# Chunk attention followed by a SoLU feed-forward layer: the start's order written anew in finer pieces, the scaling of six tiles' probabilities moved to GpSimd, and fewer warming products

## The chip, the cores and the metric

The kernel runs on one core of one Trainium2 chip. The metric is the device time of one execution in microseconds (us), the median of several runs.

## The reference

The first part is attention in chunks of 64 positions: no position sees another chunk. Its output, heads side by side, is the input of a feed-forward layer whose activation is SoLU (h times its own softmax) with a normalisation behind it.

```python
# q, k, v: 8 batches x 8 heads x 576 positions x 64 (float32)
scores = (1 / sqrt(64)) * matmul(q_c, k_c^T)              # per chunk of 64
attn   = exp(scores - max(scores)); attn = attn / (sum(attn) + 1e-9)
out    = matmul(attn, v_c)
x      = out as 4608 tokens x 512
h      = x @ w_in                                         # 512 -> 1024
solu   = h * (exp(h - max(h)) / (sum(exp(h - max(h))) + 1e-9))
ln     = (solu - mean(solu)) / sqrt(var(solu) + 1e-6) * g_ln
result = ln @ w_out                                       # 1024 -> 512
```

The weights w_in and w_out come as 64-bit floats.

## The kernel before, in words

The 4608 tokens are 36 tiles of 128. One tile holds two chunks of 64 positions. Every tile passes through the same steps, and the kernel names each step with a letter. `n` loads q and k of a tile, `v` loads v. `N:i:0` and `N:i:1` turn q and k of tile i on TensorE (four 128x128 transposes each into a bank of PSUM) and evict them to qT and kT. `S` makes the scores. `A` subtracts the maximum (VectorE) and takes the exp (ScalarE), `B` sums, inverts and scales with the inverse. `T` turns the probabilities on TensorE and ScalarE evicts them to attn_t in four copies; from tile 6 on `U` turns them on VectorE and brings them to attn_t with eight DMA loads (four issued by SyncE, four by GpSimd). `V` multiplies with v and splits the result into a high part x_h (an eviction with rounding) and a low part x_l (a subtraction on VectorE).

`M` is the input product of a tile: 24 matmuls of 512 columns, since x and w_in are each split into a high and a low part and three of the four pairings are summed. `X` takes the maximum of its 1024 sums (h_nmax, VectorE) and the exp (ScalarE). `Y` multiplies sums and exp on VectorE (z, with its sum) and then shifts by the mean on ScalarE, or on GpSimd where the step is listed. `R` forms the variance: eps and sq on ScalarE, then the tiny u and r on GpSimd. The turned z comes by TensorE for tiles 0 and 1 (`z`) and from tile 2 on by VectorE (`Z`, z_b) and 16 DMA loads to z_t. `F` is a third of the output product, 8 matmuls of 24, and `o` scales and stores a tile.

The weights come in eight pairs of rows, `P:0` to `P:7` (four of w_in, four of w_out). For each pair x, `c:x` clamps the high words of the 64-bit floats (w_a, on GpSimd) and lets ScalarE shift their range (Prelu); `b:x` converts the low words (w_b); `C:x` joins both (w_a, VectorE); `t:x` rounds to the high part (ScalarE), `d:x` subtracts for the low part (VectorE). `G` makes g_sb from g_ln. `w:n` issues n warming products on TensorE, which multiply the identity matrix and are not used.

Everything up to tile 5's input product is written out as a list of such words, `START` (lines 18 to 31). A word that appears again resumes its step where it yielded. Each engine works through its instructions strictly in the order in which the list makes them, and so does each DMA queue. `MOVED` (lines 34 to 37) names the steps that run on another engine than usual. The nat buffer that `n` fills has two places, so a load of tile i waits until tile i-2 is turned. Behind the list, from line 775 on, a loop over tiles 5 to 35 runs two tiles per turn, and each input product is followed by the scores and values of coming tiles and by thirds of an output product.

The functions that the steps of the change touch are `load_natural`, `load_v`, `turn_natural`, `unit_high`, `unit_low`, `softmax_a`, `softmax_b`, `ffn_in` and `warm`.

Of the kernel before, what the change touches and what calls it, by code (L numbers as in the profile page):

```python
# [15 lines left out]


START = """
n:0 w:3 N:0:0 N:0:0 w:1 N:0:1 N:0:1 g w:1 S:0 A:0 G P:0 P:0 n:1 A:0 c:0 c:0 w:3 N:1:0 N:1:0 w:1
N:1:1 b:0 N:1:1 G P:1 w:1 S:1 B:0 v:0 C:0 A:1 t:0 T:0 T:0 c:1 c:1 w:4 V:0 V:0 P:2 b:1 c:2 n:2  # L20
d:0 P:3 A:1 n:3 w:6 N:2:0 w:1 N:2:1 C:1 V:0 B:1 t:1 c:2 T:1 N:2:0 b:2 N:2:1 T:1 d:1 S:2 n:4
M:0 M:0 C:2 t:2 c:3 c:3 v:1 A:2 A:2 b:3 d:2 C:3 N:3:0 N:3:1 N:3:1 M:0 N:3:0 S:3 N:4:0 B:2 N:4:1
t:3 N:4:0 A:3 P:5 d:3 c:5 N:4:1 A:3 T:2 T:2 S:4 V:1 M:0 P:4 n:5 B:3 T:3 V:1 V:1 M:1 X:0 X:0 T:3
A:4 A:4 b:4 v:2 N:5:1 c:4 n:6 P:7 c:5 N:5:0 c:4 Y:0 Y:0 n:7 N:5:1 V:2 b:5 v:3 B:4 N:5:0 V:2 b:7
C:4 z:0:1 P:6 v:5 N:6:0 X:1 v:4 C:5 N:6:0 S:5 Q:2 q:8 t:4 V:2 d:4 N:6:1 N:6:1 X:1 t:5 A:5 Y:1
M:2 z:0:1 z:0:1 X:2 A:5 R:0 z:0:0 z:0:0 q:8 N:7:1 q:8 c:6 S:6 Y:1 V:3 X:2 T:4 T:4 z:0:0 d:5 F
V:3 Y:2 Y:2 N:7:0 A:6 c:6 c:7 V:3 b:6 B:5 C:6 n:8 N:7:0 M:3 R:1 c:7 q:8 N:7:1 C:7 T:5 z:1:0 t:6
T:5 S:7 t:7 d:6 X:3 X:3 d:7 V:4 V:4 Y:3 Y:3 R:2 z:1:1 A:6 F F A:7 V:4 z:1:0 z:1:0 v:6 Z:2 A:7
M:4 F B:7 Z:3 o:0 V:5 z:1:1 z:1:1 B:6 F F v:7 O:0 X:4 N:8:0 X:4 U:6 U:7 V:5 Y:4 V:5 K:9 Y:4 N:8:0
R:4 R:3 N:8:1 N:8:1 o:1  # L30
# [32 lines left out]
def chunk_attention_then_solu_ffn(  # L63
# [420 lines left out]
    def ffn_in(i):  # L486
# [2 lines left out]
        ph = st[i, "h"] = pool_h.tile([P, 2, HALF], F32, name="ph")  # L489

        sums = [(n, cc, m) for n in range(2) for cc in range(NCC) for m in range(3)]
        if i == 0:
# [388 lines left out]
```

## Time and profile before

| | |
|---|---|
| runs | 472.53, 472.22, 471.87 us; median 472.22 |
| the profiled execution | 473.01 us |
| its span (first to last instruction) | 471.2 us |
| TensorE matmuls | 461.9 us busy, 98% |
| VectorE | 374.1 us, 79% |
| ScalarE | 256.4 us, 54% |
| GpSimd | 147.6 us, 31% |
| granted TensorE clock | 1.00 in all slices |

The profile is one execution. Busy times are sums over instructions. A matmul's end is modelled and matmuls overlap, so two that follow each other in 0.23 us each show about 0.39 us. A chain of waits is followed back from the last instruction to whatever released it. A row of a timeline gives start, duration, engine, operation, what is written from what, and in brackets how long the engine stood idle before it and who ended that. Rows of one engine may overlap by some hundredths of a microsecond.

### The profile page before, as it was taken

What the parts mean: (1) busy time and instruction counts of PE and PEld (TensorE: products, weight loads), DVE (VectorE), ACT (ScalarE), POOL (GpSimd) and SP (SyncE); (2) the same over time, 40 slices, a digit from 0 to 9 for tenths busy, and PEclk for the clock granted to TensorE, in tenths of its full rate; (3) what the DMA queues carried; (4) which work ended last, traced back from release to release, by engine and by line L of the source; (5) the groups of instructions that cost most, each with busy time, mean ns of one, the idle gap of its engine ahead of it and who ended that gap; (6) DMA issues with size and microseconds to landing.
All of it is one profiled execution on the core that took longest, in us unless ns stands there. A gap on an engine that the chain in (4) does not pass through costs nothing.

```text
span 471.2 us, 11062 instructions
## 1 busy us (share of the span) xinstructions
PE 461.9 (98%) x4212; PEld 380.9 (81%) x4212; DVE 374.1 (79%) x521; ACT 256.4 (54%) x422; POOL 147.6 (31%) x298
## 2 busy tenths in 40 slices
PE   8999999999999999999999999999999999999997
PEld 6677778788888888888888888888888888888886
DVE  3999999797869887878788878797979797954441
ACT  2979984555544646464645455554555554545451
POOL 2212716151505050505050505042514141424430
PEclk9999999999999999999999999999999999999999
DMA  9999999878786878687258496948743535343231
GB/s 244 313 278 217 216 138 179 176 184 150 194 140 170 154 181 162 167 154 177 70 144 167 134 175 157 180 126 173 160 112 105 121 91 136 85 118 96 73 95 50
DMA packets 192924, 72.57 MB, mean 154 GB/s; under 512 B 177188, under 2 KB 177960, under 8 KB 191976
## 3 DMA queue, kind: packets, MB, share of 16 engines
q1 hardware_dynamic: 186200, 58.89, 57.3%
q0 software_dynamic: 6528, 12.86, 10.3%
q8 instruction: 33, 0.54, 0.5%
q14 instruction: 19, 0.16, 0.1%
q10 hardware_dynamic: 144, 0.13, 0.1%
HBM read 36.70 MB, written 9.44 MB: 98 GB/s over the span
## 4 chain that ended last, share of the span: by engine, by line
PE 85%; DMA 5%; DVE 3%; ACT 3%; SPq 2%; issue 1%; DVEq 0%; ACTq 0%
PE po L54 39%; PE ph L54 37%; PE tp L54 5%; PE sx L54 4%; SPq L54 2%; DMA nat<-in_q_dram 2%; DMA v_sb<-in_v_dram 2%; ACT z L54 1%; DMA attn_t<-a_b 1%; ACT attn_t L54 1%; ACT wo_h L54 1%; DVE z_b L54 1%; DVE z L54 0%; DVE s_sum L54 0%; ACT sq L54 0%
## 5 line engine op out<-in xcount | busy, mean ns | idle before, releaser
L54 ACT ACTIVATE z<-ph,h_nmax 128x1024 f32<-128x1024 f32 x36 | 40.2, 1118 | 139.1 <-DVE h_nmax L54 139.1
L54 PE MATMUL po<-wo_l,z_h 128*128 128x512 f32 (+1 forms) x288 | 113.0, 392 | 0.0
L54 PE MATMUL ph<-wi_l,x_h 128*128 128x512 f32 x288 | 112.8, 392 | 0.0
L54 PE MATMUL ph<-wi_h,x_h 128*128 128x512 f32 x288 | 112.2, 389 | 0.0
L54 PE MATMUL po<-wo_h,z_l 128*128 128x512 f32 (+1 forms) x288 | 111.6, 388 | 0.0
L54 PE MATMUL po<-wo_h,z_h 128*128 128x512 f32 (+1 forms) x288 | 111.4, 387 | 0.0
L54 POOL DMA_DIRECT2D z_t<-z_b x144 | 71.8, 506 | 27.0 <-DVE z_b L54 21.9
L54 PE MATMUL ph<-wi_h,x_l 128*128 128x512 f32 x288 | 78.1, 390 | 0.0
L54 POOL TENSOR_TENSOR u<-ssq,eps 128x1 f32<-128x1 f32 x36 | 6.8, 189 | 213.3 <-ACT sq L54 213.1
L54 DVE TENSOR_REDUCE h_nmax<-ph 128x1 f32<-128x1024 f32 x36 | 44.0, 1222 | 31.3 <-PE ph L54 31.2
L54 PEld LDWEIGHTS ph<-wi_h,x_l 128*128 128x128 f32 x288 | 53.9, 188 | 11.6 <-DVE x_l L54 0.4
L54 PEld LDWEIGHTS po<-wo_l,z_h 128*128 128x128 f32 x288 | 54.1, 188 | 11.4
L54 PEld LDWEIGHTS ph<-wi_l,x_h 128*128 128x128 f32 x288 | 54.1, 188 | 11.5 <-ACT x_h L54 0.2
L54 PEld LDWEIGHTS po<-wo_h,z_l 128*128 128x128 f32 x288 | 54.1, 188 | 11.1
L54 PEld LDWEIGHTS ph<-wi_h,x_h 128*128 128x128 f32 x288 | 54.1, 188 | 11.0
L54 PEld LDWEIGHTS po<-wo_h,z_h 128*128 128x128 f32 x288 | 54.1, 188 | 10.5
L54 DVE TENSOR_TENSOR z_l<-z_t,z_h 128x1024 fp32r<-128x1024 f32 (+1 forms) x37 | 42.0, 1136 | 20.9 <-ACT z_h L54 17.7
L54 DVE SCALAR_TENSOR_TENSOR z<-ph,z 128x1024 f32<-128x1024 f32 x36 | 44.1, 1224 | 13.3 <-ACT z L54 13.2
L54 ACT ACTIVATE z<-z,z_sum 128x1024 f32<-128x1024 f32 x33 | 38.1, 1155 | 22.9 <-DVE z L54 21.7
L54 DVE STREAM_TRANSPOSE z_b<-z 128x1024 f32<-128x1024 f32 x34 | 41.2, 1212 | 7.2 <-DMA v_sb<-in_v_dram 3.3
L54 ACT CAST z_h<-z_t 128x1024 fp32r<-128x1024 f32 (+1 forms) x37 | 36.0, 972 | 8.5 <-PE po L54 4.9
L54 ACT ACTIVATE o_sb<-po,r 128x512 f32<-128x512 f32 (+1 forms) x36 | 24.3, 674 | 24.7 <-POOL r L54 18.6
(76 smaller groups left out, 589.8 us busy)
## 6 DMA issues: line engine op xcount, KB each, us to landing
out_dram<-o_sb SPq DMA_DIRECT2D x35, 256.0 KB, 2.5
v_sb<-in_v_dram SPq DMA_DIRECT2D x32, 256.0 KB, 4.3
z_t<-z_b POOLq DMA_DIRECT2D x128, 64.0 KB, 2.8
z_t<-z_b SPq DMA_DIRECT2D x128, 64.0 KB, 3.0
q_st<-in_q_dram SPq DMA_DIRECT2D x96, 72.0 KB, 3.3
k_st<-in_k_dram SPq DMA_DIRECT2D x96, 72.0 KB, 3.1
w_raw<-in_moe_w_out_dram SPq DMA_DIRECT2D x4, 1024.0 KB, 7.5
attn_t<-a_b POOLq DMA_DIRECT2D x60, 64.0 KB, 3.8
```

The source lines that it names most:

```text
L54: ins = make(*args, **kwargs)
```

## The change

- The list for tiles 0 to 8 is written anew. The order of every engine and of the DMA queues changes up to tile 5's input product; the loop behind it stays.
- Steps yield more often, so that the list can put other words between their parts: `softmax_a` (between maximum and subtraction), `softmax_b` (after the sum and after the inverse), `unit_high` and `unit_low` of a pair of w_out (between their two halves), `ffn_in` of tiles 1 to 4 (every six products, as tile 0 before). Tile 1's products are sorted like tile 0's, by rows of w_in, and within these the products with x_l last. In the loop the same steps run as a whole.
- `softmax_b` scales on GpSimd for tiles 0 to 5 (`B:i=pool`).
- Evictions of N:0:1, N:2:0, V:0 and V:5 go to VectorE; those of N:0:0, N:8:0 and N:8:1 go to ScalarE. Conversion b:5 goes to GpSimd and b:7 to VectorE. The shift by the mean of tile 2 goes to GpSimd, that of tile 1 to ScalarE.
- 11 warming products instead of 21, all into one accumulator tile.
- `queue_of` could move loads to another queue; no load is listed in `MOVED`, so all stay on SyncE.

```diff
 START = """
-n:0 w:3 N:0:0 N:0:0 w:1 N:0:1 N:0:1 g w:1 S:0 A:0 G P:0 P:0 n:1 A:0 c:0 c:0 w:3 N:1:0 N:1:0 w:1
...
+n:0 P:0 P:0 c:0 w:1 w:1 w:1 n:1 w:1 N:0:0 N:0:0 N:0:1 n:2 c:0 w:1 N:0:1 S:0 A:0 A:0 b:0 P:1 N:1:0
...
 MOVED = """
-N:0:0=dve N:8:0=dve N:8:1=dve Y:0=pool Y:1=pool Y:3=pool b:7=pool c:0=pool c:1=pool c:2=pool
-c:3=pool c:4=pool c:5=pool c:6=pool c:7=pool
+Y:0=pool Y:3=pool c:0=pool c:1=pool c:2=pool c:3=pool c:4=pool c:5=pool c:6=pool c:7=pool N:0:1=dve
+B:0=pool V:0=dve N:2:0=dve B:1=pool B:2=pool B:3=pool b:5=pool B:4=pool Y:2=pool B:5=pool V:5=dve
 """
...
+    def queue_of(word):
+        return {"pool": pool, "act": act}.get(moved.get(word), sync)
...
             for y in range(2):
+                if y:
+                    yield
                 g = g_sb[:, 2 * m + y:2 * m + y + 1]
...
         dve.tensor_reduce(
             out=nmax, in_=sv, axis=AX.X, op=ALU.max, negate=True
         )
+        yield
...
         dve.tensor_reduce(out=ssum, in_=ES[i % 2], axis=AX.X, op=ALU.add)
+        yield
         rinv = small.tile([P, H], F32, name="s_rinv")
         dve.reciprocal(out=rinv, in_=ssum)
+        yield
         a = st[i, "e"] = work.tile([P, H, CH], F32, name="s_e") if i < PE_TURNED else e
-        dve.tensor_tensor(
+        (pool if f"B:{i}" in moved else dve).tensor_tensor(
             out=a, in0=e, in1=rinv.unsqueeze(2).to_broadcast([P, H, CH]), op=ALU.mult,
         )
...
-        if i == 0:
-            sums.sort(key=lambda s: s[1])
+        if i < 2:
+            sums.sort(key=lambda s: (s[1], s[2] == 2))
...
-            if i == 0 and at and at % 6 == 0:
+            if i < first and at and at % 6 == 0:
                 yield
...
+    warmed = []
+
     def warm(n):
         m = ident.unsqueeze(1).to_broadcast([P, 2, P])
-        ph = ps_h.tile([P, 2, HALF], F32, name="ph")
+        if not warmed:
+            warmed.append(ps_h.tile([P, 2, HALF], F32, name="ph"))
+        ph = warmed[0]
```

ScalarE at the very beginning, before (kT is N:0:1's eviction, e0 the exp of tile 0, w_a the Prelu of pair 0, qT and the second kT the evictions of tile 1):

```order
L54 COPY kT_111<-tp_120 128x512
L54 ACTIVATE e0_97<-e0_97 128x8x64
L54 ACTIVATE w_a_157<-w_a_157 128x1024
L54 COPY qT_164<-tp_166 128x512
L54 COPY kT_165<-tp_174 128x512
L54 CAST wi_h_90<-w_a_157 128x1024
```

The same place with the change (qT_118 is N:0:0's eviction, qT_159 and kT_160 are those of tile 1):

```order
L55 COPY qT_118<-tp_120 128x512
L55 ACTIVATE w_a_109<-w_a_109 128x1024
L55 COPY qT_159<-tp_161 128x512
L55 ACTIVATE e0_97<-e0_97 128x8x64
L55 COPY kT_160<-tp_167 128x512
L55 CAST wi_h_90<-w_a_109 128x1024
```

The exp of tile 0 moved from ahead of the Prelu to behind it and behind the eviction of N:1:0.

SyncE's DMA issues at the seam between list and loop, before (z_t are the loads of tiles 2 and 3, attn_t those of tiles 6 and 7):

```order
L54 DMA k_st<-in_k_dram 32x18x32 x8
L54 DMA v_sb<-in_v_dram 128x8x64
L54 DMA z_t<-z_b 32x512 x8
L54 DMA v_sb<-in_v_dram 128x8x64
L54 DMA out_dram<-o_sb 128x512
L54 DMA attn_t<-a_b 32x512 x4
```

With the change:

```order
L55 DMA k_st<-in_k_dram 32x18x32 x16
L55 DMA z_t<-z_b 32x512 x8
L55 DMA attn_t<-a_b 32x512 x4
L55 DMA v_sb<-in_v_dram 128x8x64
L55 DMA out_dram<-o_sb 128x512 x2
```

The load of v and the first store moved from ahead of the attn_t loads to behind them.

GpSimd at the same seam, before (u and r of tile 2 stand first, those of tiles 4 and 3 follow behind the loads):

```order
L54 TENSOR_SCALAR z<-z,z_sum 128x1024
L54 TENSOR_TENSOR u<-ssq,eps 128x1
L54 TENSOR_TENSOR r<-u,mhalf 128x1
L54 DMA z_t<-z_b 32x512 x8
L54 DMA attn_t<-a_b 32x512 x4
```

With the change (s_e is the scaling of tile 5):

```order
L55 TENSOR_TENSOR s_e<-e_98,s_rinv 128x512
L55 TENSOR_SCALAR z<-z,z_sum 128x1024
L55 DMA z_t<-z_b 32x512 x8
L55 TENSOR_TENSOR u<-ssq,eps 128x1
L55 TENSOR_TENSOR r<-u,mhalf 128x1
L55 TENSOR_TENSOR u<-ssq,eps 128x1
L55 TENSOR_TENSOR r<-u,mhalf 128x1
L55 DMA attn_t<-a_b 32x512 x4
```

u and r of tiles 2 and 3 moved between the z_t loads and the attn_t loads.

## Rows read from the trace of the kernel before

**Rows 1.** Chain of waits, end of the start: start us, us, what.

```profile
83.17 3.18 DMA attn_t<-a_b
...
88.55 5.69 PE po L54 x24
```

**Rows 2.** TensorE's timeline: start us, us, operation, count, idle before and its releaser.

```profile
16.39 2.86 PE L54 MATMUL ph<-ident 128*128 128x256 f32 x12
...
79.18 0.48 PE L54 MATMUL ph<-wi_l,x_h 128*128 128x512 f32 x1
...
84.81 0.69 PE L54 MATMUL sx<-kT,qT 64*64 64x64 f32 x32
86.59 0.96 PE L54 MATMUL sx<-attn_t,v_sb 64*64 64x64 f32 x29 [1.09 <-DMA attn_t<-a_b]
```

**Rows 3.** SyncE's timeline of DMA issues: start us, us of issuing, count.

```profile
0.73 0.45 SPq L54 DMA_DIRECT2D nat<-in_q_dram  x1
...
76.05 5.07 SPq L54 DMA_DIRECT2D z_t<-z_b  x8
...
82.59 2.43 SPq L54 DMA_DIRECT2D attn_t<-a_b  x4
```

**Rows 4.** GpSimd's timeline: pairs 2 and 6 of the weights, and attn_t.

```profile
17.47 1.57 POOL L54 TENSOR_SCALAR w_a<-w_raw 128x1024 f32<-128x1024 f32 x1 [2.66 <-DMA w_raw<-in_moe_w_in_dram]
...
52.76 1.15 POOL L54 TENSOR_SCALAR w_a<-w_raw 128x1024 f32<-128x1024 f32 x1 [0.78 <-DMA w_raw<-in_moe_w_out_dram]
...
77.73 1.97 POOL L54 DMA_DIRECT2D attn_t<-a_b  x4 [0.54 <-issue]
```

**Rows 5.** Stretches: us, busy us of PE, PEld, DVE, ACT, POOL; clock, DMA, GB/s.

```profile
466.00:472.00 6.00, 1.88 (x16) 1.67 (x14) 0.48 (x1) 0.47 (x1) 0.00 (x0) 1.00 0.12 44
...
13.59:78.54 64.95, 63.02 (x664) 50.69 (x664) 63.00 (x89) 51.28 (x93) 24.14 (x27) 1.00 1.02 220
```

**Rows 6.** VectorE's timeline, rows of the first exp, of tile 2's scaling, of tile 4.

```profile
9.65 0.16 DVE L54 TENSOR_SCALAR g_sb<-tp 128x8 f32<-128x8 f32 x1
...
11.84 1.23 DVE L54 SCALAR_TENSOR_TENSOR w_a<-w_a,w_b 128x1024 uint32<-128x1024 uint32 x1 [0.27 <-ACT w_a L54]
13.59 0.69 DVE L54 TENSOR_REDUCE s_nmax<-sx 128x8 f32<-128x512 f32 x1 [0.52 <-PE sx L54]
...
28.13 0.69 DVE L54 TENSOR_TENSOR s_e<-e,s_rinv 128x512 f32<-128x512 f32 x1
28.74 0.68 DVE L54 TENSOR_REDUCE s_nmax<-sx 128x8 f32<-128x512 f32 x1
...
77.31 1.23 DVE L54 SCALAR_TENSOR_TENSOR z<-ph,z 128x1024 f32<-128x1024 f32 x1
...
80.28 0.66 DVE L54 COPY qT<-tp 128x512 f32<-128x512 f32 x1
```

**Rows 7.** ScalarE's timeline: tile 0's exp, N:1:0's eviction, tile 4's exp, tile 3's sq.

```profile
9.17 0.63 ACT L54 ACTIVATE e<-e 128x512 f32<-128x512 f32 x1 [2.27 <-DVE e L54]
...
11.72 0.57 ACT L54 COPY qT<-tp 128x512 f32<-128x512 f32 x1
...
76.07 1.12 ACT L54 ACTIVATE z<-ph,h_nmax 128x1024 f32<-128x1024 f32 x1 [6.69 <-DVE h_nmax L54]
...
81.05 1.06 ACT L54 ACTIVATE sq<-z 128x1024 bf16<-128x1024 f32 x1
```

**Rows 8.** DMA issues of the whole run: count, KB each, median us to landing.

```profile
v_sb<-in_v_dram SPq DMA_DIRECT2D x32, 256.0 KB, 4.3
...
w_raw<-in_moe_w_in_dram SPq DMA_DIRECT2D x3, 1024.0 KB, 8.9
nat<-in_q_dram SPq DMA_DIRECT2D x8, 256.0 KB, 6.4
```

**Rows 9.** Groups by form, 0 to 88.5 us: busy us, mean ns, idle before.

```profile
L54 POOL TENSOR_SCALAR w_a<-w_raw 128x1024 f32<-128x1024 f32 x8 | 10.0, 1252 | 28.4 <-DMA w_raw<-in_moe_w_in_dram 13.2 <-DMA w_raw<-in_moe_w_out_dram 11.0 <-DVE w_a L54 4.1
...
L54 POOL TENSOR_TENSOR r<-u,mhalf 128x1 f32<-128x1 f32 x5 | 3.8, 766 | 0.4
```

More of the change, by code (lines that the diff above doesn't have):

```diff
@@ L25 @@
[L25 to L30, printed above, removed]
+n:0 P:0 P:0 c:0 w:1 w:1 w:1 n:1 w:1 N:0:0 N:0:0 N:0:1 n:2 c:0 w:1 N:0:1 S:0 A:0 A:0 b:0 P:1 N:1:0
@@ new lines @@
+w:1 N:1:1 C:0 N:2:0 n:3 N:1:0 A:0 B:0 N:1:1 S:1 N:2:0 w:1 v:0 B:0 B:0 A:1 A:1 t:0 d:0 P:2 N:2:1 w:1
+T:0 N:2:1 A:1 B:1 S:2 g T:0 v:1 c:1 c:1 w:1 P:3 B:1 A:2 N:3:0 n:4 w:1 N:3:1 N:3:0 A:2 B:1 T:1 A:2
+b:1 C:1 N:3:1 t:1 V:0 B:2 n:5 P:4 T:1 S:3 V:0 c:2 c:2 B:2 V:0 w:1 d:1 c:3 G v:2 M:0 b:2 V:1 C:2 V:1
+V:1 M:0 M:1 t:2 b:3 c:3 A:3 G N:4:0 A:3 N:4:0 M:1 C:3 N:4:1 N:4:1 N:5:0 S:4 B:2 d:2 T:2 N:5:0 Q:2
+P:5 N:5:1 A:4 t:3 d:3 M:0 M:0 M:1 A:3 A:4 T:2 B:3 c:4 A:4 N:5:1 B:3 b:4 n:6 c:4 X:0 X:0 C:4 V:2 n:7
@@ new lines @@
+S:5 Y:0 v:3 V:2 B:3 T:3 T:3 Y:0 V:2 M:1 A:5 X:1 t:4 B:4 M:2 t:4 z:0:0 P:6 z:0:0 N:6:0 X:1 v:4 A:5
+A:5 N:6:0 c:5 c:5 M:2 M:2 v:5 P:7 z:0:0 Y:1 d:4 b:5 d:4 q:8 C:5 N:6:1 z:0:1 N:6:1 z:0:1 M:2 N:7:1
+X:2 B:4 R:0 t:5 N:7:1 V:3 B:4 d:5 X:2 z:0:1 n:8 Y:2 S:6 v:6 F V:3 V:3 N:7:0 c:6 A:6 Y:1 b:6 B:5 t:5
+c:7 N:7:0 q:8 c:6 C:6 T:4 M:3 M:3 z:1:0 d:5 q:8 M:3 A:6 M:3 T:4 S:7 t:6 d:6 t:6 A:6 d:6 c:7 V:4 b:7
+C:7 R:1 t:7 t:7 X:3 d:7 F V:4 z:1:1 d:7 z:1:0 Y:2 B:5 X:3 z:1:0 B:5 F F z:1:1 A:7 Y:3 V:4 A:7 Z:2
+A:7 q:8 T:5 z:1:1 B:6 Y:3 B:7 B:7 B:6 Z:3 T:5 B:6 M:4 M:4 R:2 M:4 M:4 X:4 X:4 B:7 V:5 V:5 R:3 N:8:1
@@ L221, in unit_high @@
         else:
-            top = wo_h[:, 2 * m:2 * m + 2, :]
+            top = tops[x] = wo_h[:, 2 * m:2 * m + 2, :]
             for y in range(2):
+                if y:
+                    yield
                 g = g_sb[:, 2 * m + y:2 * m + y + 1]
@@ L238, in unit_low @@
         for y in range(2):
+            if y:
+                yield
             dve.scalar_tensor_tensor(
@@ L320, in load_natural @@
             for p0, p1, b, s in tile_parts(i):
-                sync.dma_start(
+                queue_of(f"n:{i}").dma_start(
                     nat[p0:p1, i % 2, x],
@@ L328, in load_v @@
         for p0, p1, b, s in tile_parts(i):
-            arriving[i // 2].insert(0, sync.dma_start(
+            arriving[i // 2].insert(0, queue_of(f"v:{i}").dma_start(
                 V[i][p0:p1], v[b, :, s:s + p1 - p0, :].rearrange("h t d -> t h d")
@@ L441, in attn_turn @@
                         to, of = c * CH + x * 32, c * CH + y * 32
-                        arriving[i // 2].append((pool if x == y else sync).dma_start(
+                        arriving[i // 2].append((pool if x == y else queue_of(f"U:{i}")).dma_start(
                             AT[to:to + 32, y].rearrange("p s h t -> p (s h t)"),
@@ L468, in start_softmax @@
     def start_softmax(i):
-        softmax_a(i)
+        yield from softmax_a(i)
         yield
@@ L789, in chunk_attention_then_solu_ffn @@
                 softmax_e(i + 3)
-                softmax_b(i + 3)
+                whole(softmax_b(i + 3))
                 attn_turn(i + 3)
@@ L813, in chunk_attention_then_solu_ffn @@
             if i + 3 < NT:
-                softmax_a(i + 3)
+                whole(softmax_a(i + 3))
                 softmax_e(i + 3)
@@ L828, in chunk_attention_then_solu_ffn @@
             if i + 3 < NT:
-                softmax_b(i + 3)
+                whole(softmax_b(i + 3))
                 attn_turn(i + 3)
@@ L845, in chunk_attention_then_solu_ffn @@
         if odd and i + 4 < NT:
-            softmax_a(i + 4)
+            whole(softmax_a(i + 4))
     while queue:
```

7 lines of the change are left out of this document (2 added, 5 removed).

## The prediction

> **What bounds it now.** I read the table of stretches, then the chain of waits, then each engine's timeline at the seams. The change touches only the start: everything up to tile 5's input product is written out in the list, and the loop behind it is the same code. From the first output product of the loop at 88.55 us the chain is TensorE alone [rows 1], so what the change is worth is the shift of that moment. The moment is set by V:6 (the values of tile 6) at 86.59 us: TensorE stands 1.09 us for attn_t, whose transfer lands at 86.35 us [rows 1, 2]. Three things meet there: TensorE, free for V:6 about 0.53 us after the scores at 84.81 us [rows 2]; the four attn_t loads of SyncE [rows 3]; and the four of GpSimd [rows 4].
>
> Behind TensorE stands VectorE. Between 13.59 and 78.54 us it is busy 63.00 of 64.95 us, TensorE 63.02 [rows 5]; both are nearly full. M:5 at 79.18 us [rows 2] may not begin before solu_b has read tile 4's sums, which VectorE does from 77.31 us for 1.23 us [rows 6]: to 78.54 us. So a gain must come through VectorE, M:5 and attn_t.
>
> **Warming.** Ten products fewer. Six take 2.86 us in twelve records [rows 2], so 0.48 us each, 4.8 us in all. All 21 stand ahead of M:0, the first product with weights, where TensorE waits for loads and evictions (the twelve records end at 19.25 us, and pair 2 of the weights lands at 17.47 [rows 4]). Cost and gain: 0; what ends there is a load, not a product. If the clock fell, see the rivals.
>
> **VectorE's work up to tile 4's z.** Six scalings leave; each holds the engine 0.61 us (28.13 to 28.74 us [rows 6]): -3.66. Three evictions come (N:2:0, V:0, V:5; N:0:1 takes the place of N:0:0, and b:5 and b:7 change places): a copy is 0.66 us [rows 6] less the 0.08 by which such rows overlap, so 3 x 0.58 = +1.74. N:8's two evictions leave it, but they stood behind 78.54 us and count nothing here. Sum **-1.9**.
>
> **The first exp.** On ScalarE, A:0's exp (9.17 us [rows 7]) now stands behind the Prelu of pair 0 and the eviction of N:1:0. The Prelu is done when that eviction begins at 11.72 us [rows 7]; the exp then begins 0.57 us later, at 12.3, some 3 us late. VectorE has nothing else from 9.65 us until the join of pair 0 at 11.84 us [rows 6], so it stands 2.2 us, against 0.27 and 0.52 us now [rows 6]: **+1.4**.
>
> **Weights later.** Two natural loads (tiles 2 and 3) move ahead of pairs 1 and 2 in SyncE's queue. Pair 2 lands at 17.47 us now and pair 6 at 52.76 [rows 4]. With 1024 KB a pair and 256 KB for each of q, k and v of a tile [rows 8], 4352 and 13312 KB lie up to there, counted from the first issue at 0.73 us [rows 3]: 260 and 256 KB per us. In the new list 5376 KB end with pair 2 and 6656 with pair 3: 21.4 to 21.7 us and 26.3 to 26.7 us. VectorE reaches the join of pair 2 at about 25.0 us (10.4 us of rows from 14.6 us) and that of pair 3 at 28.9. GpSimd's c (1.25 us [rows 9]) and a Prelu of about 1.0 lie between landing and join: ready at 23.9 and 28.9 at the latest. So bounds of 0 (never waits) and 4 us (the whole delay of pair 2, 17.5 to 21.5); I take **+0.6**, near the lower end, since both joins are just met.
>
> So tile 4's z ends where it ended: -1.9 + 1.4 + 0.6 = +0.1.
>
> **The scalings on GpSimd.** No row shows that operation there. Half of a c (1024 elements) is 0.63 us; a whole c, which is the upper end where VectorE works beside it, 1.57 us (17.47 us [rows 4, 9]). I take 1.1, an undisturbed c nearly, as two inputs are read instead of one. Only B:0, B:4 and B:5 have TensorE right behind them, and there M:0, M:3 and M:4 wait for VectorE anyway: 0, at the upper end +0.3. The Trainium skill, GPSIMD Engine Reference, Specifications, says that GpSimd shares its SBUF interfaces with VectorE and contends with instructions that have two SBUF inputs. By that rule the scalings would lie at the upper end, and the sum would be 0.3 us worse; the c of 1.57 us agrees with it.
>
> **M:5.** N:8's eight turns stand between the last third and M:5 now, and move ahead of the last two thirds. M:5 waits 0.64 us after z today (79.18 - 78.54) and would follow at once: **-0.5**, and TensorE is ready for V:6 at 84.81 - 0.5 + 0.1 + 0.53 = 84.9 us.
>
> **attn_t.** On SyncE its four loads stand behind the z_t loads (76.05 us for 5.07 us), a v load and a store, and begin at 82.59 us [rows 3]. The v load and the store move behind them. They begin at 81.12, 1.47 us earlier, and land at 84.9 instead of 86.35: just when TensorE is ready. The bytes of q_st and k_st ahead of them are the same, so the queue gets there at the same time. On GpSimd the four loads begin at 77.73 us [rows 4] now, and in the new order stand behind u and r of tiles 2 and 3. Those need sq of tile 3, which runs at 81.05 us [rows 7] now, but moves to right behind tile 4's exp (76.07 us for 1.12 now [rows 7]), from about 77.4 to 78.5 us; u and r take about 1.0 (r 0.77 [rows 9]), so the issues begin near 79.5, 1.8 us late, and with 2.0 of issuing [rows 4] and 3.2 of transfer [rows 1] the last lands near 84.7. V:6 then begins at about 85.1 instead of 86.59 us.
>
> **Sum: -1.5 us.** The profiled execution took 473.0 us; 471.5 on it. It lies 0.8 above the median of 472.22, so the forecast is **470.7 us**. About 0.2% (0.94 us) is what a measurement of this kernel can tell from no change; -1.5 is 0.3%.
>
> **Rivals.**
> (1) *GpSimd's loads become the wait; slower.* If sq of tile 3 stays at 81.05 us, u and r end at about 83.1, and the last of the four loads lands at 83.1 + 2.0 + 3.2 = 88.3: V:6 at 88.5, +1.9, **474.1**; each microsecond that sq comes sooner takes one off. For it: ScalarE is in order, and tile 4's exp in front of sq waits for VectorE. Against: eps and sq of tile 3 then stand ahead of the evictions of N:8 and of the Identity. It decides once the first issue begins after 79.7 us, and the gain is gone at 81.2. 0.17.
> (2) *Nothing moves.* The transfers before attn_t run later as the pairs do (P:7 goes from the seventh place to the eighth), and V:6 begins at 86.6 as now: **472.2**. 0.19.
> (3) *More.* No join waits, and SyncE's q_st and k_st issues start 1 us earlier: z at -0.5, M:5 at -1.0, attn_t at -2.5: **469.7**. Against: the queue is full of the same bytes. 0.13.
> (4) *The clock.* The granted clock is 1.00 in every stretch, even in the last, where TensorE works 1.88 of 6.00 us [rows 5]. If it fell to the lower of its levels between 7 and 23 us, the work there (32 turns, three scores, two turns of probabilities, one values: some 6.6 us by the pace of now) would double, half of it beside loads: +3.3 - 1.5, **474.0**. The Trainium skill, TensorE: Matmul & The Clock Gate, Part 1, states that the clock is throttled by default and that activity releases it; that rule speaks against fewer warming products. By that rule this case would be likely, while the last stretch does not agree with it: 0.06.
>
> **Chances and range.** The forecast has 0.45, its own range 470.0 to 471.6; some 0.37 of that lies below 471.28. Faster: 0.37 + 0.13 = 0.50. Same: 0.08 + 0.17 = 0.25 (part of rival 2 ends outside). Slower: 0.17 + 0.06 + 0.02 = 0.25. The range runs from 469.2 (beyond rival 3) to 473.8 (most of rival 1; also pairs 2 and 3 landing 3 us later than worked out, which takes the gain and 1.5 more).
>
> **What would show it.** Right: V:6 at 85.1 us with no idle for attn_t; VectorE idle about 2 us near 10 us; pair 2's c near 21.5 us; tile 4's z ending at 78 to 79 us; the scalings on GpSimd 0.6 to 1.6 us; first output product of the loop near 87.0. Wrong: a wait of VectorE above 2 us for w_a between 20 and 30 us, a wait of TensorE for attn_t above 0.5 us, GpSimd's attn_t issues after 81 us, or a granted clock below 1.00.

## The result, and the profile after

The changed kernel takes **476.35 us** (median of 4 runs, 475.68 to 477.38) against 472.17 (471.87 to 472.53): ratio 1.009, interval 1.0071 to 1.011. The forecast was 470.7, its range ended at 473.8. Timed again later, in five other rounds, the same kernel took 473.8 us (471.84 to 477.84, 12 runs) against 472.19, ratio 1.0044 (1.0023 to 1.0065). So it is slower by 0.2 to 1.1%, and its executions spread over 6 us, where those of the kernel before spread over 2.6 in the same rounds. That spread is part of what has to be explained.

| | before | after |
|---|---|---|
| the profiled execution | 473.01 us | 476.32 us |
| its span | 471.2 us | 474.5 us |
| first output product of the loop | 88.48 us | 91.41 us |
| span behind that | 382.7 us | 383.1 us |

The start costs 2.9 of the 3.3 us of span. TensorE's timeline of the changed kernel (start us, us, operation, count, idle before and its releaser), the seam that answers to [rows 2], and two rows near 10 us:

```profile
7.76 0.69 PE L55 MATMUL sx<-kT,qT 64*64 64x64 f32 x32 [0.44 <-DVE kT L55]
10.11 1.06 PE L55 MATMUL tp<-ident,nat 128*128 128x128 f32 x4 [1.65 <-DMA nat<-in_q_dram]
...
80.14 0.39 PE L55 MATMUL ph<-wi_l,x_h 128*128 128x512 f32 x1
...
83.51 1.20 PE L55 MATMUL ph<-wi_h,x_l 128*128 128x512 f32 x4 [1.40 <-DVE x_l L55]
...
88.80 0.63 PE L55 MATMUL sx<-attn_t,v_sb 64*64 64x64 f32 x27 [0.63 <-DMA attn_t<-a_b]
...
90.78 0.69 PE L55 MATMUL tp<-attn_t,v_sb 64*64 64x64 f32 x32 [0.82 <-DMA v_sb<-in_v_dram]
91.41 0.50 PE L55 MATMUL po<-wo_l,z_h 128*128 128x512 f32 x1
```

Three waits stand at the seam in place of one: M:5 for x_l (1.40), V:6 for attn_t (0.63), V:7 for its v (0.82). VectorE's timeline shows what x_l waited for: kT's turn, which stood 1.75 us for k_st loads of SyncE.

```profile
78.59 1.18 DVE L55 SCALAR_TENSOR_TENSOR z<-ph,z 128x1024 f32<-128x1024 f32 x1
...
82.17 0.71 DVE L55 STREAM_TRANSPOSE kT<-k_st 128x512 f32<-128x512 f32 x1 [1.75 <-DMA z_t<-z_b]
82.80 0.65 DVE L55 TENSOR_TENSOR x_l<-sx,x_h 128x512 fp32r<-128x512 f32 x1
```

(The row names z_t, the DMA that landed last; what the turn reads is k_st, whose sixteen issues end at 79.28 us, below.) So all three waits are for loads; M:5's wait for x_l has no term in the prediction. SyncE's issues (start us, us of issuing, count), to be held against [rows 3]:

```profile
3.78 0.61 SPq L55 DMA_DIRECT2D nat<-in_k_dram  x1
6.09 2.45 SPq L55 DMA_DIRECT2D nat<-in_q_dram  x1
8.63 0.94 SPq L55 DMA_DIRECT2D nat<-in_k_dram  x1
9.62 1.06 SPq L55 DMA_DIRECT2D w_raw<-in_moe_w_in_dram  x1
...
17.64 0.85 SPq L55 DMA_DIRECT2D w_raw<-in_moe_w_in_dram  x1
...
51.36 8.03 SPq L55 DMA_DIRECT2D q_st<-in_q_dram  x8
...
68.48 10.80 SPq L55 DMA_DIRECT2D k_st<-in_k_dram  x16
79.39 5.24 SPq L55 DMA_DIRECT2D z_t<-z_b  x8
84.80 2.41 SPq L55 DMA_DIRECT2D attn_t<-a_b  x4
87.25 0.58 SPq L55 DMA_DIRECT2D v_sb<-in_v_dram  x1
```

z_t starts at 79.39 instead of 76.05 us, attn_t at 84.80 instead of 82.59 (forecast: 81.12). The lateness begins at 4 us: the loads of tile 2 (6.09 and 8.63) wait until TensorE has turned tile 0, SyncE issues nothing from 4.39 to 6.09 us, and the second pair of weights behind them leaves at 9.62 us; in the kernel before it left at 4.71:

```profile
4.08 0.58 SPq L54 DMA_DIRECT2D nat<-in_k_dram  x1
4.71 3.89 SPq L54 DMA_DIRECT2D w_raw<-in_moe_w_in_dram  x1
```

The table of stretches shows fewer bytes behind that (us, busy us of PE, PEld, DVE, ACT, POOL; clock, DMA share, GB/s). Before:

```profile
8.00:12.00 4.00, 3.41 (x18) 2.34 (x18) 3.53 (x8) 1.88 (x3) 1.68 (x1) 1.00 1.12 287
12.00:16.00 4.00, 3.34 (x59) 2.62 (x62) 3.45 (x5) 3.58 (x8) 1.14 (x1) 1.00 1.07 374
16.00:20.00 4.00, 3.81 (x49) 3.09 (x42) 3.88 (x6) 3.83 (x5) 1.57 (x1) 1.00 1.17 290
```

After:

```profile
8.00:12.00 4.00, 2.35 (x39) 1.96 (x31) 2.88 (x4) 1.86 (x3) 1.09 (x1) 0.77 1.08 211
12.00:16.00 4.00, 4.00 (x51) 3.16 (x50) 3.34 (x7) 2.50 (x5) 1.04 (x1) 0.81 0.96 300
16.00:20.00 4.00, 2.77 (x44) 1.76 (x42) 3.86 (x6) 2.99 (x7) 2.11 (x2) 1.00 0.80 169
```

Twelve microseconds at (287 + 374 + 290) / 3 = 317 GB/s before, at 227 after: 4 x (951 - 680) = 1084 KB fewer, the size of a pair of weights. The DMA engines are hardly less busy until 16 us (share 1.08 and 0.96 against 1.12 and 1.07), and clearly less only from 16 to 20 (0.80 against 1.17); so waiting is not all of it, and why busy engines moved less isn't shown. The same rows show the lower clock (0.77 and 0.81; 0.54 from 10 to 12 us), which the profiled execution of the kernel before shows nowhere. GpSimd's timeline shows the weights late: pair 2 arrives at 25.07 (forecast: 21.4 to 21.7), pair 3 at 29.54 (26.3 to 26.7). A scaling takes 1.04 to 1.51 us there.

```profile
14.70 1.04 POOL L55 TENSOR_TENSOR s_e<-e,s_rinv 128x512 f32<-128x512 f32 x1 [4.62 <-DVE s_rinv L55]
17.83 1.10 POOL L55 TENSOR_SCALAR w_a<-w_raw 128x1024 f32<-128x1024 f32 x1 [2.09 <-DMA w_raw<-in_moe_w_in_dram]
...
25.07 2.19 POOL L55 TENSOR_SCALAR w_a<-w_raw 128x1024 f32<-128x1024 f32 x1 [5.13 <-DMA w_raw<-in_moe_w_in_dram]
29.54 1.14 POOL L55 TENSOR_SCALAR w_a<-w_raw 128x1024 f32<-128x1024 f32 x1 [2.28 <-DMA w_raw<-in_moe_w_in_dram]
30.62 1.51 POOL L55 TENSOR_TENSOR s_e<-e,s_rinv 128x512 f32<-128x512 f32 x1
```

### The profile page after: what moved, and what is told of

It reads as the page before. It is cut to its first block, busy times and chain, and to the rows that moved or that the text cites. A ratio compares the mean times of both kernels' runs of the same rounds, so it can differ in the third digit from the quotient of the medians.

```text
span 474.5 us, 11037 instructions
## 1 busy us (share of the span) xinstructions
PE 460.7 (97%) x4192; PEld 378.7 (80%) x4192; DVE 372.0 (78%) x516; ACT 255.2 (54%) x421; POOL 153.6 (32%) x304
## 4 chain that ended last, share of the span: by engine, by line
PE 88%; SPq 4%; DMA 4%; DVE 2%; issue 1%; DVEq 0%
PE po L55 40%; PE ph L55 39%; PE tp L55 5%; SPq L55 4%; PE sx L55 4%; DMA nat<-in_q_dram 3%; DMA v_sb<-in_v_dram 1%; DMA k_st<-in_k_dram 1%; DVE e L55 0%; DVE w_b L55 0%; DVE s_sum L55 0%; DVE w_a L55 0%; DVE z L55 0%; DVE s_nmax L55 0%; DVE wi_l L55 0%
## 5 line engine op out<-in xcount | busy, mean ns | idle before, releaser
L55 ACT ACTIVATE o_sb<-po,r 128x512 f32<-128x512 f32 (+1 forms) x36 | 24.2, 672 | 26.3 <-POOL r L55 19.2
```

The source lines that it names most:

```text
L55: ins = make(*args, **kwargs)
```

## The experiments

Every time is a median, every ratio is to the kernel before, timed on the same chip in the same rounds. Where the text compares kernels from different rounds, it says so.

**The seam, loads by another queue.** a_act: tile 6 and 7's attn_t loads of SyncE and tile 7's v load are issued by ScalarE. a_act_xl: also x_l of tile 5 ahead of the 32x32 turns (K:9).

```diff
+U:7=act v:7=act
```
```diff
-N:8:0 K:9 Y:4 F o:0 O:0 F V:5 N:8:0
+N:8:0 V:5 K:9 Y:4 F o:0 O:0 F N:8:0
```

> The changed kernel, with the load of v of tile 7 and SyncE's four attn_t loads issued by ScalarE. Theory 'seam' (the end of the start is set by SyncE's string of 48 issues, with v of tile 7 the very last): V:7 no longer waits for v, attn_t lands before M:5 ends at 87.4 us, the first output product of the loop comes at about 89.7 instead of 91.47 us, so about 1.8 us faster than the changed kernel (474.5). Theory 'GpSimd' and theory 'clock' (VectorE or TensorE arrive late by themselves): less than 0.6 us faster.

> As a_act, and tile 5's x_l ahead of the turns of tile 9 (K:9) on VectorE. Theory 'seam': M:5 no longer stands 1.40 us for x_l, which is hidden as long as attn_t is later but shows here: a further 1.4 us off a_act, about 473.1. If SyncE's issues still end last, or VectorE's work before tile 4's z: no further gain.

Measured: 476.19 us, ratio 1.0087 (1.0066 to 1.0107); and 477.42, 1.0117 (1.0088 to 1.0146). Neither helps. In a_act's profile neither V:6 nor V:7 waits and the first output product comes at 88.16 us (after: 91.41), though part of that is the execution's (its first z_t left at 76.04). But ScalarE does nothing else for 6.42 us around its issues, its shift of z comes at 83.16 us instead of 79.83, and the loop's first output products wait 1.4 us for z_h and z_l: the span behind that moment is 384.9 us instead of 383.1.

```profile
83.16 1.15 ACT L55 ACTIVATE z<-z,z_sum 128x1024 f32<-128x1024 f32 x1 [6.42 <-DMA attn_t<-a_b]
```

In a_act_xl S:8 stands 4.70 us for qT, an eviction that ScalarE makes behind its DMA issues: a load given to a busy engine's queue holds up what is behind it there.

**The scalings back on VectorE.** a_dve; aw_dve is the same with the three warming products of the next experiment.

```diff
-B:0=pool V:0=dve N:2:0=dve B:1=pool B:2=pool B:3=pool b:5=pool B:4=pool Y:2=pool B:5=pool V:5=dve
+V:0=dve N:2:0=dve b:5=pool Y:2=pool V:5=dve
```

> The changed kernel with the six scalings back on VectorE. Theory 'GpSimd' (beside GpSimd's work w_b and wo_l take up to 1.6 and 1.0 us each instead of 0.69 and 0.70, in all 2 us more, as much as the move saves): VectorE's rows become short again where no other GpSimd work lies beside them, tile 4's z ends within 1 us of 79.7 us, time within 1 us of 476.35. If the move really saves VectorE its 3.66 us: tile 4's z 3 us later, time 2 to 3 us slower. Theory 'seam': the same time, since SyncE's issues end last.

> The changed kernel with the three warming products behind the scores of tile 0 (474.0 us with them alone) and with the scalings of tiles 0 to 5 back on VectorE. Theory 'GpSimd's scalings cost': they lengthen VectorE's own rows beside them and stand between the weights' c, and taking them back gains 0.5 to 1 us (473.0 to 473.5), as putting them alone into the kernel before cost 0.8 to 1.0. Rival 'VectorE is full': z of tile 4 ends 3 us later and the time rises to 475 or more. Rival 'hidden': within 0.3 us of 474.0.

Measured: 475.71, 1.0083 (1.0063 to 1.0103); and 477.33, 1.0105 (1.0083 to 1.0126), against 1.0041 and 1.0034 for the same list with the scalings on GpSimd (a_warm, a_warm2 below): 0.64 to 0.71%, some 3 us, between different rounds. a_dve by itself, beside 1.009 and 1.0044 for the changed kernel, shows no such loss against the first and 1.8 us against the second. VectorE's timeline of aw_dve has tile 4's z 4.3 us later than after's:

```profile
82.91 1.19 DVE L55 SCALAR_TENSOR_TENSOR z<-ph,z 128x1024 f32<-128x1024 f32 x1
```

So the new order seems to need its scalings on GpSimd; aw_xl_v7 and aw_xl_v7_dve below, again from different rounds, lie 0.64% apart in the same direction. Alone they are another matter:

**Only the scalings.** b_pool, the kernel before with B:0 to B:5 on GpSimd.

```diff
-dve.tensor_tensor(
+(pool if f"B:{i}" in moved else dve).tensor_tensor(
...
-c:3=pool c:4=pool c:5=pool c:6=pool c:7=pool
+c:3=pool c:4=pool c:5=pool c:6=pool c:7=pool B:0=pool B:1=pool B:2=pool B:3=pool B:4=pool B:5=pool
```

> The kernel before with one edit: the scaling of the probabilities of tiles 0 to 5 runs on GpSimd. Theory 'the scalings alone pay': VectorE loses 3.66 us of rows and gains up to 2 us by contention, z of tile 4 ends 1 to 2 us earlier, and the time falls by 0 to 0.5 us, since attn_t still lands near 86.3 (471.5 to 472). Rival 'GpSimd is in order': the scalings stand behind the weights' c, and the c behind them, so T and V come later and the time rises by 0.5 to 2 us (472.5 to 474).

Measured: 473.34, 1.0022 (1.0005 to 1.004): slower by about 1 us. Tile 4's z ends at 79.79 us instead of 78.54. The groups by form (busy us, mean ns, idle before) of VectorE and GpSimd, 9 to 80 us, suggest why:

```profile
L54 DVE SCALAR_TENSOR_TENSOR w_a<-w_a,w_b 128x1024 uint32<-128x1024 uint32 x8 | 10.7, 1336 | 1.5 <-ACT w_a L54 1.5
L54 DVE SCALAR_TENSOR_TENSOR wo_l<-w_a,g_sb,wo_h 128x512 fp32r<-128x512 f32 x8 | 6.5, 850 | 0.0
L54 DVE TENSOR_REDUCE s_nmax<-sx 128x8 f32<-128x512 f32 x8 | 5.5, 685 | 3.4 <-PE sx L54 3.4
...
L54 POOL TENSOR_TENSOR s_e<-e,s_rinv 128x512 f32<-128x512 f32 x6 | 8.2, 1365 | 9.1 <-DVE s_rinv L54 9.0
```

w_a took 1221 ns and wo_l 748 in the kernel before (1221 and 779 in before2, below). VectorE stands 3.4 us ahead of s_nmax, against 1.0 in the kernel before; but before2 shows 2.8 there, so little of that is the scalings'. A scaling that held VectorE 0.61 us takes 1.365 on GpSimd, and VectorE's rows are longer where GpSimd works too; that this and the longer way of one tile use up the gain is argued, not shown by a run of its own.

**The clock.** a_warm is the changed kernel with three warming products more, b_warm the kernel before with three fewer, at the same place (behind the scores of tile 0).

```diff
-S:0 A:0 A:0 b:0
+S:0 w:3 A:0 A:0 b:0
```

> The changed kernel with three more warming products behind the scores of tile 0, where TensorE stood 1.65 us and the granted clock fell to 0.54 between 10 and 14 us. Theory 'clock': clock 1.00 throughout, the turns of tiles 1 and 2 in 0.6 instead of 1.06 us, tile 1's turn done 0.9 us sooner, hence SyncE's load of tile 3 sooner; the start ends 1 us sooner, about 475.3. Theory 'seam': clock back, start's end within 0.4 us of 91.47.

> The kernel before with one edit: the three warming products that stand behind the scores of tile 0 and the transposes of g_in (six records of 1.56 us at 7.91 us) are left out; nothing else moves. Theory 'clock': TensorE then stands about 2 us ahead of the turns of tile 1 at 10.06 us, as it does in the changed kernel (1.65 us there); the granted clock falls to about 0.5 behind that in at least some executions, and the time rises by 1 to 2.5 us in the median (473 to 474.4). Rival 'the warming products are worth something only in the new order': clock 1.00, time 471.7 to 472.5.

Measured: a_warm 474.02, 1.0041 (1.0026 to 1.0056), its profile at 1.00 throughout; this looked like 2.3 us for the clock, against the 476.35 of other rounds. b_warm 472.99, 1.002 (1.0003 to 1.0038), its profiled clock 1.00. The test was then to time both in the same rounds:

> The changed kernel, unchanged, timed in five rounds. If the 476.35 of the result is the kernel's own, the median lies between 475.5 and 477 and 471.84 is the far end of its spread. Rival: the changed kernel is as the kernel before on some chips, median 471.5 to 473.5, with the clock fallen all the same; then the clock's fall is not what costs the time.

> The changed kernel with three warming products behind the scores of tile 0, beside the one above. Theory 'clock': 1.5 to 3 us below it, with few executions below a clock of 0.999. Rival 'the clock is not the cause': the same median within 0.7 us.

Measured: **473.8 and 473.81 us**. The three products are worth nothing here; the 2.3 us were a difference between rounds. But that does not price the clock, because the fall belongs to the execution and not to the kernel. A mean granted clock below 0.999 stands beside 7 of the 12 executions of after3, 4 of the 12 of a_warm2, all four of the result (0.992 to 0.996), and 5 of the 12 of b_warm, against 1 of the 35 of the kernel before in b_warm's rounds. The 7 of after3 are 1.0 us longer than its other 5 (means 474.58 and 473.59), the 4 of a_warm2 2.3 us; in 14 of the 15 kernels (the one before aside) that show both kinds the fallen ones are longer, by 1.5 us in the mean with the kernels kept apart. In b_warm the 7 without a fall have a median of 472.23, no longer than the kernel before. Whether the fall makes an execution long, or late loads do both (TensorE stands 1.65 us ahead of the fall in after), no run shows. The 5 of after3 at full clock have a median of 473.57, 1.4 us above the kernel before: that part of the loss is there without the clock.

A fall need not cost anything. In after3 and in another execution of the changed kernel the clock falls at the same place (stretches 10 to 12 and 12 to 14 us: 0.60 and 0.55), and that other one, after2, took 471.84:

> The changed kernel, unchanged, for a second profile. If the fall of the clock comes from its order, TensorE stands 1.5 to 2.5 us ahead of the turns of tile 1 near 10 us again, the granted clock is about 0.5 behind it, M:5 waits over 1 us for x_l, and V:7 0.5 us or more for v. Rival: another stretch shows the lower clock.

after2's TensorE at the seam and SyncE, clock fallen and no loss:

```profile
84.67 0.69 PE L55 MATMUL sx<-kT,qT 64*64 64x64 f32 x32
85.19 0.75 PE L55 MATMUL sx<-attn_t,v_sb 64*64 64x64 f32 x29
...
86.67 0.70 PE L55 MATMUL tp<-attn_t,v_sb 64*64 64x64 f32 x32 [0.20 <-DMA v_sb<-in_v_dram]
87.30 0.50 PE L55 MATMUL po<-wo_l,z_h 128*128 128x512 f32 x1
```
```profile
51.07 6.31 SPq L55 DMA_DIRECT2D q_st<-in_q_dram  x8
...
75.14 5.29 SPq L55 DMA_DIRECT2D z_t<-z_b  x8
80.60 2.54 SPq L55 DMA_DIRECT2D attn_t<-a_b  x4
```

Its weights were late as well: the second pair left at 9.35 us, pairs 2 and 3 arrived at 23.59 and 28.09. Still tile 4's z ended at 78.42 us, no later than the kernel before's 78.54.

**The seam with the clock kept.** aw_xl is a_warm with x_l ahead of the turns, aw_xl_v7 has also tile 7's v load on ScalarE, aw_xl_v7_dve also the scalings on VectorE (edits as above).

> The changed kernel with the three warming products behind the scores of tile 0 (as in the run before it, 474.0 us) and with the last part of tile 5's values (the subtraction that gives x_l) ahead of the 32x32 turns that follow N:8 on VectorE. Theory 'x_l behind the turns': M:5 no longer stalls 1.9 us for x_l, and 0.5 to 1.5 us are gained (472.5 to 473.5). Rival 'SyncE's string of loads sets the end': M:5's stall goes, but TensorE waits the same time later for attn_t and z_t, and the time stays at 473.6 to 474.4.

> The same, and tile 7's v load is issued by ScalarE in place of SyncE, so that it no longer stands behind the four attn_t loads. Theory 'v load behind attn_t': V:7's wait of 0.8 us goes, and 0.3 to 0.8 us are gained on the same without it. Rival 'hidden': V:7 doesn't wait in the run without it either, because TensorE comes there later; no difference, or 0.2 worse where ScalarE's next activation is held up.

> The changed kernel with all four parts undone that are suspected: the three warming products back, x_l of tile 5 ahead of the 32x32 turns, tile 7's v load issued by ScalarE, scalings on VectorE. Theory 'these four are the loss': 472.0 to 472.8 us, about the kernel before (the same list without the scalings taken back gave 473.5). Rival 'the new order itself costs': 473.2 or more, whatever is taken back.

Measured: 474.02, 1.0038 (1.002 to 1.0056); 473.49, 1.0033 (1.0016 to 1.0051); 477.09, 1.0097 (1.0078 to 1.0117). In aw_xl M:5 no longer stands, but the same loads are waited for later:

```profile
85.39 0.29 PE L55 MATMUL sx<-attn_t,v_sb 64*64 64x64 f32 x2 [0.17 <-DMA attn_t<-a_b]
86.24 0.63 PE L55 MATMUL sx<-attn_t,v_sb 64*64 64x64 f32 x27 [0.55 <-DMA attn_t<-a_b]
...
88.05 0.69 PE L55 MATMUL tp<-attn_t,v_sb 64*64 64x64 f32 x32 [0.66 <-DMA v_sb<-in_v_dram]
```

The rival 'SyncE's string of loads sets the end' gave the number of aw_xl. aw_xl's median hides two kinds: the 8 executions at full clock lie between 472.5 and 474.61 us, the 4 with a fallen one between 474.81 and 476.87.

**The prediction's own step at the seam.** b_v7 is the kernel before with tile 7's v load on ScalarE and O:0 behind attn_t; before2 is the kernel before again.

```diff
-F F v:7 O:0 X:4 N:8:0 X:4 U:6 U:7
+F F v:7 X:4 N:8:0 X:4 U:6 U:7 O:0
```

> The kernel before with one edit at its seam: tile 7's v load is issued by ScalarE, and the store O:0 stands behind the four attn_t loads of SyncE, which so begin some 1.5 us earlier. Theory 'attn_t sets the moment' (a step of the prediction, here alone): V:6 begins at 85.4 to 85.6 us in place of 86.59 with no idle time, and the time falls by 0.5 to 1.1 us (471.1 to 471.7). Rival 'another wait takes its place': V:6 or V:7 waits for v or for z_t's parts, 472.2.

> The kernel before, unchanged, for a second profile. If the wait of 1.09 us for attn_t at 86.59 us, on which the prediction's gain rested, is the kernel's own, it is there again at 0.8 to 1.4 us. Rival: it belongs to that one execution (473.0 us, 0.8 above the median), and V:6 begins here 0.5 us or more earlier with a smaller wait.

Measured: b_v7 472.4, 1.0009 (0.9995 to 1.0023), no gain, though V:6 starts at 85.47 us without idle time. before2, one run of 471.73, shows why: the wait on which the forecast rested is not there in the unchanged kernel either.

```profile
84.88 0.69 PE L54 MATMUL sx<-kT,qT 64*64 64x64 f32 x32
85.40 0.76 PE L54 MATMUL sx<-attn_t,v_sb 64*64 64x64 f32 x29
```
```profile
74.33 5.06 SPq L54 DMA_DIRECT2D z_t<-z_b  x8
```

M:5 begins within 0.07 us of where it did [rows 2]; only the loads come 1.7 us earlier, and the 1.09 us are gone. Tile 4's z ends at 78.56 us in before2 and 78.68 in b_v7, and the first output product follows 8.5 us behind in both: VectorE sets the moment there, and earlier loads gain nothing.

**The place of tile 2's loads.** aw_n2 is a_warm with `n:2` behind the second pair of weights; aw_n2w has six warming products more, behind the turns of tile 1; aw_all has also x_l ahead of the turns and tile 7's v load on ScalarE.

```diff
-N:0:1 n:2 c:0 w:1 N:0:1 S:0 w:3 A:0 A:0 b:0 P:1 N:1:0 w:1 N:1:1 C:0
+N:0:1 c:0 w:1 N:0:1 S:0 w:3 A:0 A:0 b:0 P:1 n:2 N:1:0 w:1 N:1:1 w:6 C:0
```

> The changed kernel with the three warming products back (474.0 us with them alone), and with the loads of q and k of tile 2 behind the second pair of weights in SyncE's queue, so that this pair need not wait until TensorE has turned tile 0. Theory 'weights late': the second pair's c moves from 16.6 us to about 13, the third from 23.2 to about 20, VectorE's idle time before 30 us shrinks by 1 to 2 us, z of tile 4 ends 1 to 2 us earlier, and the time falls by 0 to 0.8 us (473.2 to 474.0), since M:5 then still waits for x_l. Rival 'tile 2 later costs the same': z of tile 4 ends where it did, 474.0.

> The changed kernel with the three warming products behind the scores of tile 0, with the loads of tile 2 behind the second pair of weights, and with six more warming products behind the turns of tile 1, where TensorE otherwise stands 3.2 us for tile 2's loads. Theory 'weights late cost': with the clock kept the time falls below the 474.0 of the three products alone, to 472.5 to 473.4. Rival 'the place of the loads is worth nothing': 473.7 to 474.3.

> The same, and x_l of tile 5 ahead of the 32x32 turns, and tile 7's v load issued by ScalarE. Theory 'these are the losses': 471.7 to 472.6 us, as the kernel before or better. Rival 'something else in the new order costs a microsecond': 473.0 or more.

Measured: aw_n2 473.95, 1.0034 (1.0021 to 1.0046); **aw_n2w 472.4, 1.0013 (0.9992 to 1.0034)**; aw_all 472.93, 1.0018 (0.9998 to 1.0038). aw_n2w, like aw_all, can't be told from the kernel before, but its interval still overlaps a_warm's. In aw_n2w the second pair leaves at 4.45 us and the stretches carry 330, 235 and 318 GB/s where after carried 211, 300 and 169:

```profile
8.00:12.00 4.00, 4.00 (x53) 3.52 (x46) 3.32 (x5) 2.48 (x5) 1.11 (x1) 1.00 1.14 330
12.00:16.00 4.00, 3.49 (x47) 2.70 (x46) 1.45 (x4) 1.09 (x2) 0.01 (x1) 1.00 1.32 235
16.00:20.00 4.00, 4.00 (x55) 3.13 (x54) 3.93 (x5) 3.20 (x7) 2.16 (x2) 1.00 1.19 318
```

Over all profiled executions, 8 to 20 us, the five in the old order moved 305 to 329 GB/s, the twelve with tile 2's loads ahead 227 to 268, the three with them behind 266 to 295: the edit brings back part of the bytes. What it moves most clearly is the start of SyncE's string of loads from q_st to z_t. aw_n2, and then a_warm, which differs from it by one moved word:

```profile
49.13 7.92 SPq L55 DMA_DIRECT2D q_st<-in_q_dram  x8
```
```profile
51.75 7.03 SPq L43 DMA_DIRECT2D q_st<-in_q_dram  x8
```

aw_n2 differs from aw_n2w by the six warming products alone. In aw_n2 TensorE stands 3.23 us for tile 2's loads, and then works at the lower clock for twice as long as after does:

```profile
14.00:16.00 2.00, 1.21 (x12) 0.91 (x16) 0.08 (x1) 0.00 (x0) 0.00 (x0) 0.50 1.35 214
16.00:18.00 2.00, 2.00 (x35) 1.59 (x34) 1.67 (x4) 0.00 (x0) 1.13 (x2) 0.50 1.51 239
18.00:20.00 2.00, 2.00 (x9) 1.71 (x8) 2.00 (x2) 1.01 (x2) 1.00 (x1) 0.50 0.95 300
```

Here the clock does seem to cost: it fell in 11 of the 12 executions of aw_n2 and in 1 of the 12 of aw_n2w, and 473.95 - 472.4 = 1.55 us by the medians (one chip, different rounds), 0.21% or 1.0 us by the ratios, whose intervals overlap; in the profiled executions tile 4's z ends at 81.3 us instead of 78.3.

**All executions together.** Read from the profiled execution of each kernel:

| kernel | time, us | SyncE's first q_st | first z_t | tile 4's z ends | first output product | span less that |
|---|---|---|---|---|---|---|
| before / before2 | 473.01 / 471.73 | 50.20 / 48.20 | 76.05 / 74.33 | 78.54 / 78.56 | 88.48 / 87.08 | 382.7 / 382.8 |
| b_v7 | 471.83 | 48.96 | 74.37 | 78.68 | 87.17 | 382.9 |
| after / after2 / after3 | 476.32 / 471.84 / 477.84 | 51.36 / 51.07 / 51.91 | 79.39 / 75.14 / 80.56 | 79.77 / 78.42 / 79.92 | 91.41 / 87.30 / 92.75 | 383.1 / 382.7 / 383.3 |
| a_warm / a_warm2 | 475.05 / 476.41 | 51.75 / 52.46 | 78.83 / 79.87 | 80.03 / 81.16 | 90.53 / 91.74 | 382.8 / 382.9 |
| aw_xl | 473.19 | 51.36 | 77.00 | 78.63 | 88.67 | 382.7 |
| aw_n2 | 474.00 | 49.13 | 75.80 | 81.37 | 89.45 | 382.8 |
| aw_n2w / aw_all | 472.26 / 471.66 | 49.67 / 49.46 | 76.19 / 75.01 | 78.34 / 79.09 | 87.77 / 87.19 | 382.7 / 382.7 |

In these rows the loop behind is worth the same, to 0.6 us. The later of two things sets the moment. One is the loads: where they are later, the first output product follows the first z_t by 11.6 to 12.4 us. The other is tile 4's z: where that is later, the product follows its end by 8.5 us in the old order (before2, b_v7, b_warm, b_pool) and by 8.0 to 8.1 in the new one (aw_n2, aw_all and the kernels with the scalings on VectorE).

Tile 2's loads move the string. With them ahead of the second pair (12 profiled executions, all kernels) the first q_st leaves at 50.6 to 52.5 us; with them behind it (3) at 49.1 to 49.7; in the old order (5) at 48.2 to 50.2. z_t follows at 75.1 to 80.6, 78.0 in the mean; at 75.0 to 76.2; and at 74.3 to 76.1, 75.0 in the mean.

## Why the prediction was wrong

**The step that failed: attn_t, "the queue gets there at the same time".** The -1.5 us rests on SyncE reaching z_t at 76.05 us as before, because the bytes ahead are the same. It got there at 79.39 us, and in the mean of the twelve executions with this order of loads at 78.0, against 75.0 in the old order. So the loads, which were to hold TensorE no longer, held it more. An estimate from the table: by tile 4's z and the 8.0 us behind it the first output product of after would have come at 87.8; it came at 91.41, 3.6 us later. In the profiled kernel before the same sum (78.54 + 8.5) leaves 1.4 us for the loads. M:5's wait for x_l, 1.40 us in after and 2.9 in after3, is one that the prediction had no term for: x_l stands behind kT's turn on VectorE, and that turn waits for k_st.

**The same error earlier: weights later, +0.6 us, between 0 and 4.** The arrival of pairs 2 and 3 was worked out from bytes at 260 and 256 KB per us. SyncE issues nothing while the load at its head waits for a buffer, and 1084 KB less were moved between 8 and 20 us: the pairs came 3.5 and 3 us later than worked out, as the range's upper end foresaw ("takes the gain and 1.5 more"). But the price was not paid where the term had it, in VectorE's joins: after2, with its pairs 2 and 1.5 us late, ended tile 4's z at 78.42 us. It was paid in the string of loads at the end, which starts 2.4 us later in the mean (51.4 against 49.1). Moving tile 2's loads back brings that start to 49.4; in the time it brought the ratio from 1.0034 and 1.0041 (a_warm2, a_warm) to 1.0013 (aw_n2w), 1.0 to 1.3 us, from different rounds, with intervals that overlap, and with six warming products more. aw_n2, without these, gained nothing. So the place of the loads is shown to move the string, and only likely to be worth the time.

**What is not the order's.** SyncE goes from issue to issue from 64 to 87 us, so what it is late it mostly stays. But the string from q_st to z_t took 28.0, 24.1 and 28.7 us in the three executions of after, 25.4 to 26.1 in the five of the old order. That is where most of the 6 us of spread come from: z_t at 79.39, 75.14 and 80.56 for 476.32, 471.84 and 477.84 us. Why the string takes longer in some executions stays open, and so how much of the loss the order makes by itself.

**The gain that wasn't there.** The 1.09 us of idle time for attn_t [rows 2], which were to go, were read in an execution that took 0.8 us more than the median. before2 doesn't have them, and b_v7, which removes them, gains nothing.

**What was right.** SyncE's order of issues, GpSimd's attn_t issues (80.27 us, 79.5 forecast; no loss, since SyncE's came later), and that the moment hangs on loads. M:5's -0.5 came: where z sets the moment, the output product follows it by 8.0 to 8.1 us instead of 8.5, 0.3 of it at M:5 (0.36 us behind z in aw_n2, 0.69 in before2). The first exp ran at 11.68 us (12.3 forecast), and VectorE's idle times near it were 0.57 and 0.62 us, not 2.2: +0.4 in place of +1.4. Tile 4's z ended at 79.77 us, forecast 78 to 79 (after2: 78.42, after3: 79.92). That the v load behind attn_t costs nothing was wrong in place (V:7 stood 0.82 us for it), but taking it away gained 0.5 us at most (474.02 to 473.49, intervals overlapping).

**The scalings.** Forecast 1.1 us each, cost 0 to 0.3. They take 1.04 to 1.51, and VectorE's rows beside GpSimd's work grow (w_a 1221 to 1336 ns in b_pool; in after, 9 to 80 us, w_b 851 to 988 and wo_l 748 to 889, some 2 us in all), for which the -3.66 had no counterpart. The Trainium skill, GPSIMD Engine Reference, Specifications, says that both engines share SBUF interfaces; the trace agrees, and the price alone, in the old order, was 1 us, above the upper end. In the new order they seem to be worth some 3 us, by ratios of different rounds: the sign of such a step depends on the order around it.

**Rival 4, the clock.** It fell, as the rival said, where 0.06 had been given; its price, +3.3, no run bears out. In the sum the price was 0, and what it is in the changed kernel stays open: 1.0 us between the two kinds of execution in after3, no loss in after2, no cause shown. It is not all of the loss, since after3 is 1.4 us slower at full clock. The Trainium skill, TensorE: Matmul & The Clock Gate, Terms, puts the penalty near the throttled time times the share of clock lost: for 10 to 14 us of after 2 x 0.46 + 2 x 0.39 = 1.7 us, an estimate by that page. The 1.5 us between the kinds in 15 kernels agree in size; in aw_n2 the rule gives 2 x (0.09 + 0.5 + 0.5 + 0.5) = 3.2 us up to 20 us, where 1.0 to 1.55 was measured. There it was an upper end.

**What stays open.** aw_n2w leaves 0.3 us to the kernel before by the medians, 0.6 by the ratio, within its interval. No version beat the kernel before. That the twenty-one warming products went into fresh tiles, the eleven into one, wasn't tried by itself. In four of the six kernels with loads on ScalarE the span behind the first output product is 1.2 to 2.2 us longer; in a_act 1.4 us of it are the waits for z_h and z_l, the others weren't followed up.

## What to carry to other kernels

A queue issues nothing more while the load at its head waits for a buffer, so work out an arrival from what each load waits for, not from the bytes ahead of it alone; put loads with a free buffer ahead of those that must wait, and follow a late queue to its end, where it may cost more than at the first load that is late. Before a wait in a profile is priced as a gain, see whether a second execution has it, and what else would set the moment without it. Compare variants in the same rounds on the same chip, and look at the granted clock of every execution: equal medians said nothing about the clock as long as it fell in both kernels.

## What the runs showed of the hardware

- Executions of one kernel in the same rounds differ in the granted clock (below 0.999 in 7 of 12 of after3), and those where it fell are longer: 1.0 us in after3, 1.9 in aw_xl, 1.5 in the mean of the 15 kernels that show both. Which of the two causes the other isn't shown. In aw_n2, where it fell for some 7 us in the profile, 1.0 to 1.55 us were lost against the same kernel with six warming products more.
- The same string of loads from one queue (32 of 72 KB and three others between) took from 24.1 to 28.7 us in executions of one kernel; no row read here tells what disturbed it.
- GpSimd's scaling of 512 elements a partition with two inputs takes 1.04 us at the shortest and 2.02 beside VectorE's join of a pair (aw_n2, 30.08 us); the join beside it took 1.95 us instead of 1.23.
